# A linear-attention pair on one core: one more copy goes through the staging ring, one PSUM bank changes its ring, the launch's idle matmuls read a constant, and the order is fitted anew

## The chip, the core and the metric

The kernel runs on one core of a Trainium2 chip. The time is device microseconds of one execution, and the median of the runs is compared. The core has a matmul engine (TensorE, PE in the profile, whose weight loads are listed apart as PEld), three engines for element-wise work (VectorE is DVE, ScalarE is ACT, GpSimd is POOL), and queues that start transfers (SP is SyncE's; the other engines have queues of their own). Each engine runs its instructions strictly in the order in which they were written; they wait for one another by semaphores.

## The reference

Two independent blocks, A and B, each with its own `x` (2048 x 640), `wqkv` (640 x 1920) and `wo` (640 x 640), 32 heads of 20; the two results stand side by side in the output (2048 x 1280):

```python
q, k, v = split_heads(x @ wqkv)
phi = lambda t: jnp.where(t > 0, t + 1, jnp.exp(t)) + 1e-6
pq, pk = phi(q), phi(k)
kv = jnp.einsum("bhsd,bhse->bhde", pk, v)
z = jnp.einsum("bhsd->bhd", pk)
num = jnp.einsum("bhqd,bhde->bhqe", pq, kv)
den = jnp.einsum("bhqd,bhd->bhq", pq, z)[..., None] + 1e-6
out = merge_heads(num / den) @ wo
```

There is no softmax: keys and values meet in a 20 x 20 matrix per head, so `x` need not be multiplied by the value weights. The kernel forms G = phi(k)^T x first, then kv from G, then M = kv · wo, so that the output is (phi(q) / den) @ M.

## The kernel before, in words

**Arithmetic.** Every fp32 operand is split by a pair of passes into a high part (`xnh`, `kah`, `pkh` ..., written by ACT) and a low remainder (`xnl`, `kal`, `pkl` ..., written by DVE); a product is then three matmuls, high·high, low·high and high·low (`mm3`, lines 183 to 185, and `product`, line 333).

**First half: keys (about 0 to 290 us).** x comes in tiles of 128 rows. For each, phi(k) is found and G is added up. The projections of keys go by pairs of tiles in seven products (`STEPS`, `product`), as a block-matrix scheme that saves one product of eight; the first six tiles are projected plainly (`psk`, line 594). A product's results lie in PSUM banks "a" (`pa`), "e" (`pe`) and "one" (`psb`). ACT copies `pa` out (`ko`, line 337), DVE adds the others to it (line 340), and then follow exp (ACT), relu (ACT), min-and-add (`ek`, DVE, line 553), the high part `pkh` (ACT, line 565) and the low part `pkl` (DVE, line 569). Four tiles make a group; `gsum` multiplies the group's `pk` with its rows `xn` into a bank `psg` (seven sums, five of 512 columns and strips of 384 and 256), and DVE adds these to `gacc`. The column sums z of phi(k) are gathered by accumulating transfers (`zd`, line 561). `xn` is the row-wise load of x (`load_x`, line 406), in a ring "xr" of five buffers that it shares with `xt`, the transposed load from which `kah` and `kal` are cut.

**Between the blocks (159 to 200 us).** While block B's keys begin, block A's kv is made head group by head group: `kvmm` (`pskv`, line 776), a mask (`kvt`, line 783), its split (`kvh`, `kvl`), then `mmm` multiplies it with `wo` into two banks `psm` (80 or 120 rows), `m_out` copies both out to `mev` by ACT (line 337), and POOL stores them to DRAM as `md` (line 844). There are six head groups per block, four of 120 rows and two of 80.

**Second half: queries (about 290 to 562 us).** Eight units of 512 rows: Q by `psq`, phi(q), the denominators (`denmm`, bank `psd`, for the first and the last unit; sums by transfers for the rest), division, and `outmm` with M in the same seven products.

**What sets the order.** In the first half every step of PE and every piece of work beside it (a "job": a copy, a split, a load, a store) has a place, a number that follows from which step it feeds; `MOVED` shifts steps and `SHIFT` shifts jobs by a table of numbers, and all are then written out in the order of the places, dependencies first. In the second half `at` hangs work behind a matmul of Q or a product of the output, and `AT` shifts it by so many slots. A buffer is one of a ring named by its tag; its next user waits for the last reader of the user before it, a transfer included.

**What the change touches.** `m_out` takes `mev` of block A from ring "ek" (three buffers of pool `kg`, shared with `ek`) at this line:

```python
pool, tag, bufs = (q2[0], "o", 4) if q2 else (kg[0], "ek", 3)
```

Ring "wst" is the staging ring of seven buffers in pool `base` (`stage`): weights, `wv`, `wo` and later `md` are loaded into it. `bank` hands out PSUM banks by tag. At the launch, before any data is there, seven matmuls of bf16 on `idle`, a tile that DVE has zeroed (line 1108), go into a bank `psi` that nobody reads (line 1111).

Of the kernel before, what the change touches and what calls it, by code (L numbers as in the profile page):

```python
# [14 lines left out]
H = 32  # L15
# [7 lines left out]
    ('exp', 11): 0.74, ('exp', 13): 3.23, ('exp', 14): 0.41, ('exp', 15): 0.95, ('exp', 16): 0.91, ('exp', 18):  # L23
    -0.02, ('exp', 20): -0.96, ('exp', 22): 1.7, ('exp', 25): 0.96, ('exp', 28): 1.07, ('exp', 29): 0.86, ('exp',
    3): 4.78, ('exp', 4): 0.16, ('exp', 6): 0.87, ('exp', 8): -0.31, ('exp', 9): 2.13, ('f1', 'k', 0, 1): 0.31,
    ('f1', 'k', 1, 0): -0.71, ('f1', 'm', 0, 0): 1.2, ('f1', 'm', 0, 1): -0.83, ('f2', 'k', 0, 1): 2.5, ('f2', 'm',
    0, 0): 0.42, ('f5', 'k', 0): -0.1, ('f5', 'k', 1): -2.28, ('fdh', 'k', 1, 2): 0.51, ('fdh', 'k', 1, 4): 0.91,
# [10 lines left out]
    ('gacc', 7, 1): 0.04, ('gacc', 7, 4): 0.45, ('gacc', 7, 5): 1.7, ('gacc', 7, 6): 2.69, ('iota', 0): 0.8, ('kt',
    0): 0.53, ('kt', 1): 1.13, ('kt', 5): 5.23, ('kvh', 0): 1.2, ('kvh', 1): 5.9, ('kvh', 4): 1.1, ('kvl', 1): 2.02,
    ('kvl', 3): 2.08, ('ld', 'k', 1, 0): 0.56, ('ld', 'k', 1, 1): -0.06, ('ld', 'k', 1, 3): -9.42, ('ld', 'k', 1,  # L40
    4): -3.84, ('ld', 'm', 0, 0): 1.22, ('ld', 'm', 0, 1): 0.8, ('ld', 'm', 0, 2): 1.54, ('ld', 'm', 0, 3): -0.03,
    ('ld', 'm', 0, 4): -0.19, ('mc', 4, 1): 0.69, ('mix', 11): 0.24, ('mix', 12): 0.49, ('mix', 13): 7.61, ('mix',
    14): 4.05, ('mix', 15): -0.8, ('mix', 19): 1.66, ('mix', 2): -0.07, ('mix', 20): 0.31, ('mix', 23): 0.53,
# [1550 lines left out]
```

## Time and profile before

| | us |
|---|---|
| median of 3 runs | 568.26 (568.25 to 568.28) |
| the profiled execution | 567.32 |
| its span, first to last instruction | 565.2 |
| PE busy | 560.1 (99%) |
| PEld busy | 512.0 (91%) |
| DVE busy | 423.8 (75%) |
| ACT busy | 329.5 (58%) |
| POOL busy | 84.4 (15%) |

The profiled execution is 0.94 us shorter than the median of the runs, and 2.1 us of it lie outside the span. PE's time counts a matmul as busy up to a modelled end, so the distance from one matmul's start to the next one's says more than the busy share. A row of the timeline gives the start, the duration, the engine, the line, the operation with output<-inputs, and in brackets how long the engine had been idle before it and what ended that; where a row covers several instructions, xN says how many.

### The profile page before, as it was taken

What the parts mean: (1) busy time and instruction counts of PE and PEld (TensorE: products, weight loads), DVE (VectorE), ACT (ScalarE), POOL (GpSimd) and SP (SyncE); (2) the same over time, 40 slices, a digit from 0 to 9 for tenths busy, and PEclk for the clock granted to TensorE, in tenths of its full rate; (3) what the DMA queues carried; (4) which work ended last, traced back from release to release, by engine and by line L of the source; (5) the groups of instructions that cost most, each with busy time, mean ns of one, the idle gap of its engine ahead of it and who ended that gap; (6) DMA issues with size and microseconds to landing.
All of it is one profiled execution on the core that took longest, in us unless ns stands there. A gap on an engine that the chain in (4) does not pass through costs nothing.

```text
span 565.2 us, 9089 instructions
## 1 busy us (share of the span) xinstructions
PE 560.1 (99%) x3231; PEld 512.0 (91%) x3231; DVE 423.8 (75%) x729; ACT 329.5 (58%) x619; POOL 84.4 (15%) x141
## 2 busy tenths in 40 slices
PE   9999999999999999999999999999999999999997
PEld 7989999898989898989888899898989989898997
DVE  5987798886584878878855896968679485676892
ACT  5964676663575775666736764745547363454551
POOL 0111122311011112143110103121012101001010
PEclk9999999999999999999999999999999999999999
DMA  8969789999894787989998986846566994433022
GB/s 278 254 144 252 166 233 306 294 309 357 297 237 121 193 247 127 362 226 247 335 277 292 333 262 215 286 137 227 154 215 233 297 380 135 156 86 111 1 94 93
DMA packets 78613, 126.74 MB, mean 224 GB/s; under 512 B 9768, under 2 KB 40872, under 8 KB 78568
## 3 DMA queue, kind: packets, MB, share of 16 engines
q1 hardware_dynamic: 66120, 86.28, 47.3%
q0 software_dynamic: 12160, 39.66, 26.0%
q8 instruction: 25, 0.41, 0.3%
q10 hardware_dynamic: 288, 0.23, 0.1%
q14 instruction: 20, 0.16, 0.1%
HBM read 73.62 MB, written 49.37 MB: 218 GB/s over the span
## 4 chain that ended last, share of the span: by engine, by line
PE 96%; ACT 1%; DMA 1%; issue 0%; DVE 0%; POOL 0%; DVEq 0%; ACTq 0%
PE pa L333 22%; PE pe L333 11%; PE psq L183 8%; PE psq L185 8%; PE psq L184 8%; PE psg L184 8%; PE psg L185 8%; PE psg L183 8%; PE psb L333 7%; PE psk L594 5%; PE pskv L776 2%; DMA md<-mev 1%; PE psi L1111 1%; PE psm L183 1%; PE psm L185 1%; PE psm L184 1%
## 5 line engine op out<-in xcount | busy, mean ns | idle before, releaser
L183 PE MATMUL psq<-xqh,wqh 128*128 128x512 f32 x200 | 78.4, 392 | 0.0
L185 PE MATMUL psq<-xqh,wql 128*128 128x512 f32 x200 | 78.0, 390 | 0.0
L184 PE MATMUL psq<-xql,wqh 128*128 128x512 f32 x200 | 77.9, 389 | 0.0
L183 PE MATMUL psg<-pkh,xnh 128*128 128x512 f32 x160 | 62.8, 393 | 0.0
L184 PE MATMUL psg<-pkl,xnh 128*128 128x512 f32 x160 | 62.7, 392 | 0.0
L185 PE MATMUL psg<-pkh,xnl 128*128 128x512 f32 x160 | 62.6, 392 | 0.0
L337 ACT ACTIVATE o<-pa 128x320 f32<-128x320 f32 x64 | 28.1, 439 | 53.8 <-PE pa L333 53.6
L561 POOL DMA_DIRECT2D zd<-ek x30 | 26.1, 871 | 134.9 <-DVE ek L553 55.5
L185 PEld LDWEIGHTS psq<-xqh,wql 128*128 128x128 f32 x200 | 37.5, 188 | 7.9
L337 ACT ACTIVATE ko<-pa 128x320 f32<-128x320 f32 x52 | 22.5, 434 | 37.6 <-PE pa L333 37.4
L184 PEld LDWEIGHTS psq<-xql,wqh 128*128 128x128 f32 x200 | 37.6, 188 | 7.3
L183 PEld LDWEIGHTS psq<-xqh,wqh 128*128 128x128 f32 x200 | 37.6, 188 | 7.3
L944 ACT ACTIVATE pq<-psq 128x512 f32<-128x512 f32 x40 | 23.7, 594 | 28.0 <-PE psq L185 27.8
L185 PEld LDWEIGHTS psg<-pkh,xnl 128*128 128x128 f32 x160 | 30.0, 188 | 6.4
L998 DVE SCALAR_TENSOR_TENSOR pq<-pq,rd 128x1280 f32<-128x1280 f32 x16 | 23.4, 1483 | 16.2 <-DMA rd<-da 16.1
L184 PEld LDWEIGHTS psg<-pkl,xnh 128*128 128x128 f32 x160 | 30.1, 188 | 5.8 <-DVE pkl L569 0.5
L183 PEld LDWEIGHTS psg<-pkh,xnh 128*128 128x128 f32 x160 | 30.0, 188 | 5.2
L946 DVE SCALAR_TENSOR_TENSOR pq<-pq,rq 128x512 f32<-128x512 f32 x40 | 27.4, 686 | 8.4 <-ACT rq L945 8.4
L565 ACT ACTIVATE pkh<-ek,epst 128x640 fp32r<-128x640 f32 x32 | 26.5, 836 | 10.6 <-DVE ek L553 10.5
L553 DVE SCALAR_TENSOR_TENSOR ek<-ek,ko 128x640 f32<-128x640 f32 x32 | 26.2, 819 | 7.8 <-ACT ko L550 6.6
L639 DVE TENSOR_TENSOR gacc<-psg,gacc 128x512 f32<-128x512 f32 (+2 forms) x42 | 25.6, 627 | 6.7 <-PE psg L185 6.6
L340 DVE TENSOR_TENSOR o<-pe,o 128x320 f32<-128x320 f32 x32 | 15.3, 479 | 20.4 <-PE pe L333 13.5
(213 smaller groups left out, 1666.2 us busy)
## 6 DMA issues: line engine op xcount, KB each, us to landing
zd<-ek POOLq DMA_DIRECT2D x32, 320.0 KB, 5.3
out<-o POOLq DMA_DIRECT2D x28, 320.0 KB, 3.4
xql<-xd SPq DMA_DIRECT2D x24, 256.0 KB, 4.6
xt<-in_B_xt_tiles SPq DMA_DIRECT2D x16, 320.0 KB, 4.9
xn<-in_B_x SPq DMA_DIRECT2D x16, 320.0 KB, 5.6
xqs<-in_A_xt SPq DMA_DIRECT2D x20, 256.0 KB, 6.2
xqs<-in_B_xt SPq DMA_DIRECT2D x20, 256.0 KB, 5.7
fdmh<-fsh POOLq DMA_DIRECT2D x14, 320.0 KB, 4.5
```

Source lines behind the costliest of these rows:

```text
L183: nc.tensor.matmul(o, whi, xhi, start=first, stop=False)
L184: nc.tensor.matmul(o, whi, xlo, start=False, stop=False)
L185: nc.tensor.matmul(o, wlo, xhi, start=False, stop=last)
L333: nc.tensor.matmul(o, x, y, start=start and m == r == 0, stop=m == len(terms) - 1 and r == 2, skip_group_check=True)
L337: nc.scalar.activation(x, y, AF.Copy)
L553: nc.vector.scalar_tensor_tensor(ek[n], ek[n], 1.0, rk[n], op0=OP.min, op1=OP.add)
L561: nc.gpsimd.dma_start(zacc[b], e, accum_op=OP.add)
L565: nc.scalar.activation(pk[n][0], ek[n], AF.Identity, bias=epst)
L594: nc.tensor.matmul(kps["c", n][h], plain_x(n, c)[i], plain_w(c)[j][:, h * HF:(h + 1) * HF], start=(c == 0 and i == j == 0), stop=(c == NC ...
L639: nc.vector.tensor_tensor(o, x, o, op=OP.add)
L944: nc.scalar.activation(e, ps, AF.Exp)
L946: nc.vector.scalar_tensor_tensor(e, e, 1.0, r, op0=OP.min, op1=OP.add)
```

## The change

Three edits, and tables that were fitted again with them:

1. `m_out` takes block A's `mev` from the staging ring "wst" (seven buffers) instead of ring "ek" (three).
2. PSUM tag "small" (one bank, used by `psi` and `psd`) is gone; "one" has four banks instead of three, and `psi` and `psd` are taken from it. The total stays eight.
3. The idle matmuls read a bf16 constant 1.0 that the framework has in memory instead of `idle`; the tile and its memset go. `psi` is not read, so its value does not matter.
4. `SHIFT`, `MOVED` and `AT` have other numbers (some 300 entries in all; a few rows stand below).

```diff
@@ SHIFT, MOVED and AT: the core of it
 SHIFT = {
-    ('c0', 10): 1.79, ('c0', 11): 0.04, ('c0', 12): 0.56, ('c0', 3): 1.17, ('c0', 6): 0.26, ('c0', 7): 0.57, ('c0',
+    ('c0', 10): 1.79, ('c0', 12): 0.56, ('c0', 6): 0.26, ('c0', 7): 1.33, ('c0', 8): 0.25, ('c0', 9): 2.23, ('c2',
...
 MOVED = {
-    ('G', 2, 5): 2.0, ('G', 6, 0): 4.0, ('H', 3, 0, 0): 3.5, ('T', 1): 1.5, ('c', 2, 3): -3.0, ('m', 4): 3.0, ('p',
-    11, 3): -0.5, ('p', 13, 2): 1.0, ('p', 14, 0): -0.5, ('p', 14, 2): -2.0, ('p', 6, 1): 3.5, ('p', 7, 1): -1.0,
-    ('p', 7, 2): -2.5, ('p', 8, 4): -1.5, ('p', 9, 3): 2.0,
+    ('G', 2, 5): 2.0, ('G', 6, 0): 4.0, ('H', 3, 0, 0): 3.5, ('H', 7, 2, 2): 1.5, ('c', 2, 3): -2.5, ('c', 3, 3):
+    0.5, ('m', 5): -2.5, ('p', 13, 2): 1.0, ('p', 14, 0): -0.5, ('p', 14, 2): -2.0, ('p', 3, 6): -1, ('p', 6, 1):
+    3.5, ('p', 7, 1): -1.0, ('p', 7, 2): -2.5, ('p', 8, 4): -1.5, ('p', 9, 3): 2.0,
 }
...
     def bank(name, tag="one"):
-        return psums.tile([P, 512], F32, name=name, tag=tag, bufs={"one": 3, "a": 2, "e": 2, "small": 1}[tag])
+        return psums.tile([P, 512], F32, name=name, tag=tag, bufs={"one": 4, "a": 2, "e": 2}[tag])
...
         if h == 0:
-            pool, tag, bufs = (q2[0], "o", 4) if q2 else (kg[0], "ek", 3)
+            pool, tag, bufs = (q2[0], "o", 4) if q2 else (base, "wst", 7)
             mps[b, g, 2] = pool.tile([r, 2, HF], F32, name="mev", tag=tag, bufs=bufs)
...
     def denmm(u):
         t = acc.pop(u)
-        ps = den.pop(u) if u in den else bank("psd", "small")
+        ps = den.pop(u) if u in den else bank("psd")
...
     open_pool(kg, "kg", "left")
     open_pool(kx, "kx", "right")
-    idle = kg[0].tile([P, P], BF16, name="idle", tag="ek", bufs=3)
-    nc.vector.memset(idle, 0.0)
-    ps = bank("psi", "small")
+    idle = nc.const_aps.tensor(1.0, (P, P), BF16)
+    ps = bank("psi")
     for i in range(7):
```

The tables are 13 lines shorter, so a line number of the rows below is 13 smaller after the change (337 becomes 324).

**ScalarE where the fifth head group's M is copied out (about 194 to 198 us).** `mev<-psm 80x320 x2` are the two copies of that group, `ko<-pa` the copies of a key product's bank, `kah` and `ksh` high parts for the next products. Before:

```order
L337 ACTIVATE mev<-psm 120x320 x2
L550 ACTIVATE ko<-ko 128x640
L429 ACTIVATE kah<-xt 128x128
L805 ACTIVATE woh<-wo 80x640
L429 ACTIVATE ksh<-sx 128x512
L565 ACTIVATE pkh<-ek,epst 128x640 x2
L337 ACTIVATE ko<-pa 128x320
L337 ACTIVATE mev<-psm 80x320 x2
L337 ACTIVATE ko<-pa 128x320
```

and after:

```order
L537 ACTIVATE ko<-ko 128x640
L324 ACTIVATE mev<-psm 120x320 x2
L416 ACTIVATE kah<-xt 128x128
L792 ACTIVATE woh<-wo 80x640
L416 ACTIVATE ksh<-sx 128x512 x2
L552 ACTIVATE pkh<-ek,epst 128x640 x2
L324 ACTIVATE mev<-psm 80x320 x2
L324 ACTIVATE ko<-pa 128x320
L416 ACTIVATE ksh<-sx 128x512
L324 ACTIVATE ko<-pa 128x320
```

The 80-row copies now stand one copy of `pa` earlier. The first of them waited before for PE and for a transfer of a POOL queue (the store of an earlier `mev`, whose buffer in "ek" it takes); after, it waits for PE alone, since the buffer of "wst" that it takes was last read by DVE.

**TensorE in the last group's sums, at the third of the four tiles that it takes up (about 274 us).** `psg` are the banks of these sums, `pkh_3393` and `pkl_3394` (after: `pkh_3391` and `pkl_3392`) the two parts of that tile's phi(k), `xnh` and `xnl` those of its rows of x. Before:

```order
L183 MATMUL psg_3386<-pkh_3393,xnh_3308 128x512
L184 MATMUL psg_3386<-pkl_3394,xnh_3308 128x512
L185 MATMUL psg_3386<-pkh_3393,xnl_3309 128x512
L183 MATMUL psg_3396<-xnh_3308,pkh_3393 128x384
L184 MATMUL psg_3396<-xnl_3309,pkh_3393 128x384
L185 MATMUL psg_3396<-xnh_3308,pkl_3394 128x384
```

and after:

```order
L170 MATMUL psg_3394<-xnh_3310,pkh_3391 128x384
L171 MATMUL psg_3394<-xnl_3311,pkh_3391 128x384
L172 MATMUL psg_3394<-xnh_3310,pkl_3392 128x384
L170 MATMUL psg_3384<-pkh_3391,xnh_3310 128x512
L171 MATMUL psg_3384<-pkl_3392,xnh_3310 128x512
L172 MATMUL psg_3384<-pkh_3391,xnl_3311 128x512
```

The strip of 384 columns now comes first, so that the low part is wanted by the third matmul instead of the second.

**VectorE while block A's kv is masked (about 162 to 166 us).** `kvt` is a masked kv, `kvl` its low part, `pkl` the low parts of the first two tiles whose group sums PE takes up next. Before:

```order
L553 SCALAR_TENSOR_TENSOR ek_2003<-ek_2003,ko_1889 128x640
L173 TENSOR_TENSOR ksl_2018<-sx_1988,ksh_2017 128x512
L173 TENSOR_TENSOR kvl_2032<-kvt_2027,kvh_2031 120x120
L783 TENSOR_TENSOR kvt_2047<-pskv_2040,mask6_884 120x120
L173 TENSOR_TENSOR kal_1961<-xt_1822,kah_1960 128x512
L553 SCALAR_TENSOR_TENSOR ek_2037<-ek_2037,ko_1888 128x640
L783 TENSOR_TENSOR kvt_2067<-pskv_2061,mask4_887 80x80
L569 SCALAR_TENSOR_TENSOR pkl_2058<-ek_2003,pkh_2057 128x640
L569 SCALAR_TENSOR_TENSOR pkl_2073<-ek_2037,pkh_2072 128x640
```

and after:

```order
L160 TENSOR_TENSOR kvl_1986<-kvt_1983,kvh_1985 120x120
L540 SCALAR_TENSOR_TENSOR ek_2005<-ek_2005,ko_1884 128x640
L160 TENSOR_TENSOR ksl_2019<-sx_1988,ksh_2018 128x512
L160 TENSOR_TENSOR kvl_2033<-kvt_2028,kvh_2032 120x120
L770 TENSOR_TENSOR kvt_2051<-pskv_2044,mask6_882 120x120
L160 TENSOR_TENSOR kal_1954<-xt_1817,kah_1953 128x512
L540 SCALAR_TENSOR_TENSOR ek_2041<-ek_2041,ko_1883 128x640
L770 TENSOR_TENSOR kvt_2068<-pskv_2062,mask4_885 80x80
L556 SCALAR_TENSOR_TENSOR pkl_2058<-ek_2005,pkh_2057 128x640
L770 TENSOR_TENSOR kvt_2084<-pskv_2078,mask4_885 80x80
L556 SCALAR_TENSOR_TENSOR pkl_2076<-ek_2041,pkh_2075 128x640
```

One `kvl` has come to stand ahead of these rows and one mask multiply between the two `pkl`; both stood behind them before.

Two more places, in words. At about 209 to 212 us two `pkl` stood together before, behind an `ek`, the add of `pe` and a `kal` of 512 columns; after, the first stands ahead of all three, and the second alone behind them. And at about 50 us the load of A's rows 896 to 1023 (`xn` of tile 7) took a buffer of ring "xr" that a `kal` of 128 columns had freed; after, it takes the one of `xn` of tile 4, whose `xnl` stands on DVE right behind the add of a bank `psb`. On SyncE's queue the load stands in both between two loads of B's key weights.

More of the change, by code (lines that the diff above doesn't have):

```diff
@@ L19 @@
 SHIFT = {
[3 rows of a table removed]
[L23 to L27, printed above, removed]
@@ L28 @@
-    ('fdh', 'k', 1, 6): 0.53, ('fdh', 'm', 0, 7): 0.62, ('fdh', 'm', 0, 8): 0.57, ('fdl', 'k', 1, 1): 0.84, ('fdl',
[6 rows of a table removed]
-    ('fl', 'm', 0, 8): 1.99, ('gacc', 0, 1): 3.2, ('gacc', 1, 0): 2.35, ('gacc', 1, 3): 2.05, ('gacc', 2, 1): 2.89,
-    ('gacc', 2, 3): 0.28, ('gacc', 3, 1): 2.86, ('gacc', 3, 2): 2.86, ('gacc', 3, 3): 3.83, ('gacc', 3, 5): 2.14,
-    ('gacc', 4, 0): 0.75, ('gacc', 4, 4): 2.17, ('gacc', 5, 3): 1.28, ('gacc', 5, 5): 0.51, ('gacc', 7, 0): 0.31,
-    ('gacc', 7, 1): 0.04, ('gacc', 7, 4): 0.45, ('gacc', 7, 5): 1.7, ('gacc', 7, 6): 2.69, ('iota', 0): 0.8, ('kt',
@@ L39 @@
[L39 to L43, printed above, removed]
@@ L44 @@
-    ('mix', 26): 0.21, ('mix', 29): 2.2, ('mix', 3): -0.55, ('mix', 5): 7.49, ('mix', 7): 1.18, ('mix', 8): 4.49,
[16 rows of a table removed]
-    11): 0.09, ('relu', 13): 1.06, ('relu', 21): 4.46, ('relu', 25): 2.55, ('relu', 28): 1.48, ('relu', 30): 3.49,
[13 rows of a table removed]
-    ('wol', 4): 0.03, ('wqh', 1): 2.01, ('wql', 2): -0.55, ('wql', 4): 2.4, ('xh', 10, 'A1'): -0.17, ('xh', 10,
[13 rows of a table removed]
+    ('c0', 10): 1.79, ('c0', 12): 0.56, ('c0', 6): 0.26, ('c0', 7): 1.33, ('c0', 8): 0.25, ('c0', 9): 2.23, ('c2',
+    4): 0.43, ('c2', 8): 1.19, ('c2', 9): 0.48, ('c4', 15): 0.21, ('c5', 12): 0.75, ('c5', 3): 0.07, ('c5', 6):
@@ new lines @@
+    1.78, ('c5', 8): 1.02, ('exp', 0): 2.55, ('exp', 11): 0.74, ('exp', 13): 3.23, ('exp', 15): 0.61, ('exp', 16):
+    0.91, ('exp', 20): -0.96, ('exp', 22): 1.7, ('exp', 25): 0.96, ('exp', 28): 1.07, ('exp', 29): 1.23, ('exp', 3):
+    3.4, ('exp', 4): 2.25, ('exp', 6): 1.17, ('exp', 8): -0.31, ('exp', 9): 2.13, ('f1', 'm', 0, 0): 1.2, ('f1',
+    'm', 0, 1): -0.83, ('f2', 'k', 0, 1): 3.88, ('f2', 'm', 0, 0): 0.42, ('f5', 'k', 0): -2.36, ('f5', 'k', 1):
+    -2.28, ('fdh', 'k', 1, 2): 0.51, ('fdh', 'k', 1, 4): 0.91, ('fdh', 'k', 1, 6): 0.53, ('fdh', 'm', 0, 7): 0.57,
@@ new lines @@
+    ('fdl', 'k', 1, 1): 0.84, ('fdl', 'k', 1, 8): 1.97, ('fdl', 'm', 0, 2): 1.2, ('fdl', 'm', 0, 3): 0.76, ('fdl',
[5 rows of a table added]
+    ('gacc', 2, 1): 2.89, ('gacc', 3, 1): 2.86, ('gacc', 3, 2): 2.64, ('gacc', 3, 3): 3.78, ('gacc', 3, 5): 2.12,
+    ('gacc', 4, 0): 0.75, ('gacc', 4, 4): 2.17, ('gacc', 5, 3): 1.28, ('gacc', 5, 5): 0.51, ('gacc', 7, 0): 0.31,
+    ('gacc', 7, 5): 2.76, ('gacc', 7, 6): 1.79, ('iota', 0): 0.8, ('kt', 0): 1.7, ('kvh', 0): 1.2, ('kvh', 4): 1.1,
+    ('kvl', 1): 2.02, ('kvl', 3): 6.46, ('ld', 'k', 1, 0): 0.9, ('ld', 'k', 1, 1): -0.06, ('ld', 'k', 1, 3): -9.42,
@@ new lines @@
+    ('ld', 'k', 1, 4): -2.83, ('ld', 'm', 0, 1): 0.8, ('ld', 'm', 0, 3): -0.03, ('ld', 'm', 0, 4): -0.19, ('mc', 4,
+    1): 0.69, ('mix', 11): 0.24, ('mix', 12): 0.49, ('mix', 13): 7.61, ('mix', 14): 1.67, ('mix', 15): -0.8, ('mix',
+    17): 0.16, ('mix', 19): 1.66, ('mix', 20): 0.31, ('mix', 23): 1.04, ('mix', 29): 2.2, ('mix', 3): -0.55, ('mix',
[13 rows of a table added]
+    ('q6', 9): 0.96, ('relu', 1): 0.93, ('relu', 10): 1.37, ('relu', 11): 0.09, ('relu', 13): 1.06, ('relu', 21):
+    3.97, ('relu', 25): 2.55, ('relu', 28): 1.48, ('relu', 30): 3.62, ('relu', 5): 1.82, ('s1', 10): -0.46, ('s1',
[10 rows of a table added]
@@ L89 @@
+    9, 'h'): -5.5, ('woh', 4): 0.48, ('wol', 0): 0.5, ('wol', 3): 0.37, ('wol', 4): 0.03, ('wq', 4): -4.51, ('wqh',
[13 rows of a table added]
     'S3'): 2.46, ('xl', 8, 'A1'): 0.25, ('xl', 8, 'A5'): 1.23, ('xl', 8, 'S1'): 0.8, ('xl', 8, 'S3'): 1.04, ('xl',
[3 rows of a table removed]
[2 rows of a table added]
 }
 MOVED = {
[3 rows of a table removed]
[3 rows of a table added]
 }
@@ L102 @@
     ('a_split', 1, 0): 2, ('a_split', 2, 0): -1, ('a_split', 3, 0): -1, ('a_split', 5, 0): 2, ('a_split', 6, 0): 7,
-    ('d_split', 1, 0): 7, ('d_split', 1, 1): 5, ('d_split', 3, 1): -5, ('d_sums', 1, 0): 4, ('divide', 1, 0): 1,
-    ('divide', 2, 0): 1, ('divide', 5, 0): 1, ('form_last', 'm', 1): 5, ('form_load', 0, 5): -2, ('form_load', 1,
-    1): -2, ('form_load', 1, 5): -1, ('form_split', 'm', 1, 0): 5, ('form_split', 'm', 1, 1): -4, ('form_split',
-    'm', 1, 2): -3, ('form_split', 'm', 1, 3): -11, ('form_split', 'm', 1, 8): 3, ('form_split', 'm', 1, 9): 5,
-    ('form_sums1', 'm', 1, 1): -5, ('gather', 5): 4, ('invert', 3): -1, ('invert', 5): 3, ('kv_step', 1, 5): -2,
-    ('load_w', 'q', 1, 0): -3, ('load_w', 'q', 1, 4): 8, ('m_step', 1, 2): 1, ('m_step', 1, 3): 1, ('split_o', 1,
-    5): -2, ('split_w', 1, 0): -3, ('split_w', 1, 2): -7, ('split_w', 1, 4): 1,
+    ('d_split', 1, 1): 5, ('d_sums', 1, 0): 4, ('denmm', 0): -1, ('divide', 1, 0): 1, ('divide', 2, 0): 1,
+    ('form_last', 'm', 1): 5, ('form_split', 'm', 1, 0): 5, ('form_split', 'm', 1, 1): -4, ('form_split', 'm', 1,
+    2): -3, ('form_split', 'm', 1, 3): -11, ('form_split', 'm', 1, 8): 3, ('form_split', 'm', 1, 9): 5,
+    ('form_sums1', 'm', 1, 1): -5, ('invert', 3): -1, ('kv_step', 1, 5): -2, ('load_w', 'q', 1, 4): 8, ('m_step', 1,
+    2): 1, ('m_step', 1, 3): 1, ('split_w', 1, 0): -3, ('split_w', 1, 2): -7, ('split_w', 1, 4): 1,
 }
```

96 rows, old and new, of the table SHIFT are left out of this document.

## The prediction

> **What bounds the kernel now.** I read the page first, then PE's busy time by stretches of the span, then PE's waits, the chain of waits, and last PE's timeline at the gaps. PE is the bound:
>
> ```profile
> PE 560.1 (99%) x3231; PEld 512.0 (91%) x3231; DVE 423.8 (75%) x729; ACT 329.5 (58%) x619; POOL 84.4 (15%) x141
> ```
>
> ```profile
> core 0: us, PE busy (x) PEld busy (x) DVE busy (x) ACT busy (x) POOL busy (x), PEclk, DMA share, GB/s
> ...
> 32.00:285.00 253.00, 252.23 (x1473) 231.55 (x1472) 198.87 (x373) 158.62 (x289) 52.18 (x80) 1.00 0.88 248
> ...
> 304.00:532.00 228.00, 228.00 (x1251) 205.94 (x1251) 170.91 (x251) 126.81 (x233) 26.75 (x49) 1.00 0.61 206
> ```
>
> In the second half (304 to 532) PE has no idle time at all, in the first half (32 to 285) 0.77 us. The number of matmuls does not change, so all that the change can give lies in PE's few gaps. Two of them are named among its waits; the longest one inside stands on the chain as a transfer:
>
> ```profile
> PE psi L1111 <- DVE idle L1108: 1.0, 1, 1.0
> PE pa L333 <- ACT mev L337: 0.7, 1, 0.7
> ```
>
> ```profile
> 190.60 6.03 DMA md<-mev
> ...
> 332.60 1.76 PE pa L333 x12
> ```
>
> The second line gives the normal distance between matmuls of 320 columns, 1.76 / 12 = 0.147; for 512 columns it is 0.23 (rows at 165.83 and 166.06 below). Since idle time hides under modelled ends, I measure a gap as start to start, less that distance.
>
> **The change, part by part.**
>
> *`mev` in the staging ring.* ACT and PE at the gap:
>
> ```profile
> 196.73 0.76 ACT L337 ACTIVATE mev<-psm 80x320 f32<-80x320 f32 x2 [1.94 <-DMA md<-mev]
> ```
>
> ```profile
> 196.25 0.31 PE L333 MATMUL pa<-wfh,ksl 128*128 128x320 f32 x1
> 197.22 0.41 PE L333 MATMUL pa<-wfh,kah 128*128 128x320 f32 x1 [0.66 <-ACT mev L337]
> 197.47 0.30 PE L333 MATMUL pa<-wfl,kah 128*128 128x320 f32 x1
> ```
>
> The copy waited until the store of an earlier `mev`, issued at 190.60, had landed, and PE waited for the bank. PE loses 0.97 - 0.147 = 0.82, and the matmul behind a wait comes 0.25 after it instead of 0.147, another 0.10: 0.92 in all. After the change that store no longer owns the slot. What is late next: ACT had nothing to do for 1.94 before 196.73, so the pair could begin at 194.8 and end at 195.6, 0.8 before PE's turn at 196.25 + 0.15. The new slot was last read by DVE's split of `wo`, long ago; the next users of "wst" are the loads of `md`, which wait for all these stores anyway. POOL's store starts earlier and nobody waits for it there. So -0.92, between -0.92 and 0 (if another reader holds the slot).
>
> *Two `pkl` set apart, and the strip first.*
>
> ```profile
> 210.77 1.55 DVE L569 SCALAR_TENSOR_TENSOR pkl<-ek,pkh 128x640 fp32r<-128x640 f32 x2
> ...
> 212.12 0.40 PE L183 MATMUL psg<-pkh,xnh 128*128 128x512 f32 x1
> 212.38 0.50 PE L184 MATMUL psg<-pkl,xnh 128*128 128x512 f32 x1
> 212.72 0.40 PE L185 MATMUL psg<-pkh,xnl 128*128 128x512 f32 x1
> ```
>
> ```profile
> 273.95 0.82 DVE L569 SCALAR_TENSOR_TENSOR pkl<-ek,pkh 128x640 fp32r<-128x640 f32 x1 [0.90 <-ACT pkh L565]
> ...
> 274.49 0.40 PE L183 MATMUL psg<-pkh,xnh 128*128 128x512 f32 x1
> 274.83 0.50 PE L184 MATMUL psg<-pkl,xnh 128*128 128x512 f32 x1
> 275.17 0.40 PE L185 MATMUL psg<-pkh,xnl 128*128 128x512 f32 x1
> ```
>
> At 212 PE loses 0.60 - 0.46 = 0.14 to a `pkl` that ends at 212.32. One `pkl` now precedes in DVE's idle time, so the last ends some 0.7 earlier: -0.14. At 274 PE loses 0.68 - 0.46 = 0.22. With the strip first, `pkl` is wanted after two matmuls of 384 columns instead of one of 512, by the ratio of columns 2 x 0.17 = 0.34 instead of 0.23 later, just when it is ready (274.77): -0.22, at worst -0.11.
>
> *A copy behind a load.*
>
> ```profile
> 206.14 0.74 ACT L473 ACTIVATE xnh<-xn 128x640 fp32r<-128x640 f32 x1 [0.26 <-DMA xn<-in_B_x]
> ...
> 208.90 0.42 ACT L337 ACTIVATE ko<-pa 128x320 f32<-128x320 f32 x1
> ...
> 209.10 0.40 PE L185 MATMUL psg<-pkh,xnl 128*128 128x512 f32 x1
> 209.38 0.42 PE L333 MATMUL pa<-wfh,kah 128*128 128x320 f32 x1
> 209.63 0.31 PE L333 MATMUL pa<-wfl,kah 128*128 128x320 f32 x1
> ```
>
> PE loses 0.05 + 0.10 = 0.15 behind a copy that a load delayed by 0.26. The loads around it stand further apart in the new order, so I take -0.15; if the load lands no sooner while PE arrives 0.92 earlier, it is up to +0.77 instead.
>
> *A kv mask and a `kvl` ahead of a `pkl`.* This is the one place where the new order costs something that I can see:
>
> ```profile
> 162.07 0.28 DVE L173 TENSOR_TENSOR kvl<-kvt,kvh 120x120 fp32r<-120x120 f32 x1
> 162.26 0.27 DVE L783 TENSOR_TENSOR kvt<-pskv,mask 120x120 f32<-120x120 f32 x1
> ...
> 163.79 0.23 DVE L783 TENSOR_TENSOR kvt<-pskv,mask 80x80 f32<-80x80 f32 x1
> 163.94 1.65 DVE L569 SCALAR_TENSOR_TENSOR pkl<-ek,pkh 128x640 fp32r<-128x640 f32 x2
> ```
>
> ```profile
> 165.83 0.39 PE L184 MATMUL psg<-pkl,xnh 128*128 128x512 f32 x1
> 166.06 0.39 PE L185 MATMUL psg<-pkh,xnl 128*128 128x512 f32 x1
> ```
>
> The second `pkl` ends at 165.59. At 212 a `pkl` that ended at 212.32 held PE as if its matmul had begun at 212.49, 0.17 later; here that is 165.76, 0.07 before the turn. A `kvl` takes 0.19 of DVE (162.07 to 162.26) and a mask multiply 0.15 (163.79 to 163.94): 0.34 more, less 0.07, is +0.27; with the mask alone +0.08. I take +0.20.
>
> *The launch.* PE's first matmul waited 1.0 for the zeroed tile; without it, PE may start sooner, by less than that. But its work soon waits for data:
>
> ```profile
> 7.57 0.29 ACT L176 ACTIVATE kah<-x 128x128 fp32r<-128x128 f32 x1
> 7.92 0.56 PE L594 MATMUL psk<-wh,kah 128*128 128x320 f32 x2
> ```
>
> The matmul at 7.92 follows at once a split (7.57 + 0.29 = 7.86) that hangs on loads: what PE wins ahead of it is waited away. So 0; bounds 0 and -0.1, one wait's aftermath. [...]
>
> *The banks.* PE's waits name no `psd` or `psq`, and PE is never idle in the second half. Four banks in one ring instead of three and one: 0, with +0.1 if the last unit's `psd` delays a `psb`. The `AT` moves and the tail: 0, with PE's unbroken work as their cover.
>
> The sum: -0.92 - 0.14 - 0.22 - 0.15 + 0.20 = -1.23. Against the profiled execution that is 567.32 - 1.23 = 566.1 (565.2 of it is now span, 2.1 around it). The median of the runs stands 0.94 above the profiled one, and the change gives 568.26 - 1.23 = 567.0. A measurement of this kernel can tell about 0.2% (1.14 us) from no change; the forecast lies just beyond that.
>
> **The rivals.**
>
> *A load comes later than its copy needs it (slower).* The load of tile 7's rows gets another buffer:
>
> ```profile
> 50.57 0.33 SPq L406 DMA_DIRECT2D xn<-in_A_x  x1
> ...
> 52.42 0.49 DVE L340 TENSOR_TENSOR ko<-psb,ko 128x320 f32<-128x320 f32 x1 [1.92 <-PE psb L333]
> ...
> 57.02 0.74 ACT L473 ACTIVATE xnh<-xn 128x640 fp32r<-128x640 f32 x1 [0.27 <-DMA xn<-in_A_x]
> 58.95 0.44 ACT L337 ACTIVATE ko<-pa 128x320 f32<-128x320 f32 x1 [1.20 <-PE pa L333]
> ...
> 61.16 0.44 ACT L337 ACTIVATE ko<-pa 128x320 f32<-128x320 f32 x1 [0.22 <-PE pa L333]
> ...
> 62.34 0.31 PE L333 MATMUL pa<-wfh,ksh 128*128 128x320 f32 x1
> ```
>
> ```profile
> DMA to landing us min/median/max: 3.1/5.1/8.7
> ```
>
> It was issued at 50.57 and used at 57.02, 6.45 later. After, its buffer is freed by an `xnl` behind the add at 52.42: 52.9 + 0.8 (a DVE pass of 640 columns) = 53.7. ACT can take 1.20 + 0.22 of delay, and PE's matmul at 62.34 another 0.7 past the copy at 61.16 (ends 61.60): it must land by 57.02 + 2.1 = 59.1, within 5.4. At the median of all `xn` loads it does. With its own 6.45 it costs 1.05 + 0.10, and the sum is about -0.1: no change, 568.2. At 8.7 it costs 3.4: 570.4. It decides for slower from a landing of 5.4 + 2.3 = 7.7 on. For it speaks that transfers are busy 0.88 of that stretch, against it that SyncE has issued nothing for some 4 us by then. [...] The load of 206.14 is a second place of the same kind.
>
> *The wait only moves.* If the slot in "wst" is held, or ACT's row comes late for another reason, PE still waits at 197: the sum without the first term is -0.31, 567.9.
>
> *The kv place costs its full price and the small gains do not come.* -0.92 + 0.27 = -0.65: 567.6.
>
> **How the numbers follow.** Forecast 0.60, of which 0.48 beyond -1.14 and 0.12 short of it; a load that is late by up to some 2 us, the wait that only moves and the small gains lost, together 0.18, all within 0.2%; slower by a load near the top of its landing times, here or at 206, 0.22. Faster 0.48, same 0.30, slower 0.22. The range begins at 566.2 (the sum with +0.20 gone, the launch's -0.1 and 0.5 from moves that I did not price) and ends at 569.3, between a landing of 6.45 and one of 8.7; outside it I leave 0.2.
>
> **What would show it.** After the change the chain has no `md<-mev` near 190, PE's waits do not name `mev`, and the starts at 196 to 197 run on at 0.15. Near 274 three matmuls of 384 columns come first, with no distance above 0.25. At about 166 a matmul on `pkl` comes some 0.2 late. A first matmul well before 1.0 and an unchanged one near 7.9 show the launch right. I am wrong if ACT's `xnh` or a `ko<-pa` stands behind a transfer for more than 1.5 us near 60 or 205, or if a wait that is not in the old trace stands on the chain.

## The result and the profile after

| | before | after |
|---|---|---|
| median of 8 runs of each, us | 568.19 (566.68 to 569.24) | 566.26 (565.61 to 566.99) |
| ratio, 95% interval | | 0.997 [0.9958, 0.9981] |
| the profiled execution, us | 567.32 | 566.22 |
| its span, us | 565.2 | 564.4 |
| time outside the span, us | 2.1 | 1.8 |

The change makes the kernel 1.93 us faster, by the interval 1.1 to 2.4. The two profiled executions differ by less, 1.10, since that of before was a short one: 0.87 below the median of its kernel, that of after 0.04 below. The ratios here and below are worked out from the single runs, without three executions of 930 to 1978 us, and so need not be the ratios of the medians.

The page's first part and PE's busy time by stretches, after. The columns of the second are those that the prediction shows:

```profile
PE 560.2 (99%) x3231; PEld 512.1 (91%) x3231; DVE 424.1 (75%) x728; ACT 329.0 (58%) x619; POOL 84.4 (15%) x141
```

```profile
32.00:285.00 253.00, 252.94 (x1478) 232.19 (x1477) 201.04 (x376) 161.19 (x295) 52.23 (x80) 1.00 0.88 250
...
304.00:532.00 228.00, 228.00 (x1253) 206.00 (x1252) 171.18 (x251) 126.09 (x233) 26.76 (x49) 1.00 0.61 203
```

PE's idle time between 32 and 285 us has fallen from 0.77 to 0.06; the second half is as full as it was. Of PE's waits one is left, of 0.8 at the launch.

ACT and PE where the fifth group's M is copied out, after:

```profile
193.62 0.74 ACT L324 ACTIVATE mev<-psm 80x320 f32<-80x320 f32 x2
```

```profile
196.52 0.31 PE L320 MATMUL pa<-wfh,kah 128*128 128x320 f32 x1
196.67 0.31 PE L320 MATMUL pa<-wfl,kah 128*128 128x320 f32 x1
```

The copy waits for no transfer, and PE's starts run on at 0.15: the 0.92 of before is gone. The places where the prediction expected a loss or a remainder, PE after, at 166, 274 and (not expected) 264 us:

```profile
165.56 0.39 PE L170 MATMUL psg<-pkh,xnh 128*128 128x512 f32 x1
165.83 0.50 PE L171 MATMUL psg<-pkl,xnh 128*128 128x512 f32 x1
166.17 0.40 PE L172 MATMUL psg<-pkh,xnl 128*128 128x512 f32 x1
...
263.81 0.40 PE L171 MATMUL psg<-pkl,xnh 128*128 128x512 f32 x1
264.15 0.50 PE L172 MATMUL psg<-pkh,xnl 128*128 128x512 f32 x1
264.48 0.40 PE L170 MATMUL psg<-pkh,xnh 128*128 128x512 f32 x1
...
274.06 0.44 PE L172 MATMUL psg<-xnh,pkl 128*128 128x384 f32 x1
274.34 0.40 PE L170 MATMUL psg<-pkh,xnh 128*128 128x512 f32 x1
```

Against the usual 0.23 between matmuls of 512 columns (and 0.17 of 384), PE loses 0.04 + 0.11 at 166, 0.11 + 0.10 + 0.04 at 264 (the last from 264.95 to 265.22) and 0.11 at 274. Measured in this way, start to start, the profiled pair differs as follows:

| place, us | before | after | after - before |
|---|---|---|---|
| launch, up to the start near 8.7 (8.63 and 8.76) | | | +0.13 |
| 28 | 0.10 | 0 | -0.10 |
| 156 | 0.37 | 0.32 | -0.05 |
| 166 | 0 | 0.15 | +0.15 |
| 196 to 197 (`mev`) | 0.92 | 0 | -0.92 |
| 209 (copy behind a load) | 0.15 | 0 | -0.15 |
| 212 (`pkl`) | 0.14 | 0 | -0.14 |
| 264 | 0 | 0.25 | +0.25 |
| 274 (strip first) | 0.22 | 0.11 | -0.11 |
| sum | | | -0.94 |

The spans differ by 0.8, and what lies around the spans by 0.3.

### The profile page after: what moved, and what is told of

Same layout as the page of the kernel before. It is cut to its first block, busy times and chain, and to the rows that moved or that the text cites. A ratio compares the mean times of both kernels' runs of the same rounds, so it can differ in the third digit from the quotient of the medians.

```text
span 564.4 us, 9087 instructions
## 1 busy us (share of the span) xinstructions
PE 560.2 (99%) x3231; PEld 512.1 (91%) x3231; DVE 424.1 (75%) x728; ACT 329.0 (58%) x619; POOL 84.4 (15%) x141
## 4 chain that ended last, share of the span: by engine, by line
PE 99%; ACT 1%; DVE 0%; issue 0%; DVEq 0%
PE pa L320 22%; PE pe L320 11%; PE psg L172 8%; PE psg L171 8%; PE psg L170 8%; PE psq L170 8%; PE psq L172 8%; PE psq L171 8%; PE psb L320 7%; PE psk L581 5%; PE pskv L763 2%; PE psm L170 1%; PE psm L172 1%; PE psm L171 1%; PE psi L1097 1%; PE pst L641 0%
## 5 line engine op out<-in xcount | busy, mean ns | idle before, releaser
L416 ACT ACTIVATE ksh<-sx 128x512 fp32r<-128x512 f32 x26 | 16.2, 628 | 24.6 <-DVE sx L434 24.3
```

## The experiments

The prediction's large term is the wait of `mev`. My theory at the start was: the ring alone removes it and gives some 0.9 us, and the tables do the small rest. One rival was that the wait only moves; another that the fitted tables and the ring need each other. The first four kernels put the ring, the tables and the three edits apart. Each kernel is compared with runs of before made beside it on the same chip; the medians of before there were 567.68 (first four), 567.78 (next four) and 567.41 (last four).

| kernel | median us | ratio to before, 95% |
|---|---|---|
| e1_ring_only | 568.04 | 1.001 [0.9995, 1.0025] |
| e2_ring_back | 570.21 | 1.0044 [1.003, 1.0058] |
| e5_three_edits | 568.01 | 1.0009 [0.9994, 1.0023] |
| e6_before_again | 567.71 | 0.9996 [0.9985, 1.0006] |
| e9_ring_and_load | 568.25 | 1.0011 [1.0, 1.0021] |
| e3_const_only | 567.50 | 0.9995 [0.9984, 1.0007] |
| e4_banks_only | 567.44 | 0.9998 [0.9986, 1.001] |
| e8_three_waits | 565.56 | 0.9959 [0.9942, 0.9975] |
| e10_ring_and_z | 567.21 | 0.9989 [0.9979, 0.9999] |
| e12_ring_z_load | 565.94 | 0.9972 [0.9961, 0.9983] |
| e11_z_late | 568.27 | 1.0004 [0.9992, 1.0016] |
| e14_after_again | 565.95 | 0.997 [0.9958, 0.9981] |

### e1: the ring alone

The kernel before, with one line changed:

```diff
-            pool, tag, bufs = (q2[0], "o", 4) if q2 else (kg[0], "ek", 3)
+            pool, tag, bufs = (q2[0], "o", 4) if q2 else (base, "wst", 7)
```

> The kernel before with one edit: block A's mev from the staging ring instead of ring ek. My theory: the wait of ScalarE for md<-mev near 190 to 197 is gone, TensorE's starts run on at 0.15 there, and the kernel is 0.9 us faster than before (0.6 to 1.2), about half of what the whole change gave (1.9). Rival, the wait only moves (another reader or ScalarE's row holds TensorE at the same place): 0, within 0.3. Rival, the wait in a typical execution is longer than in the profiled one: 1.5 to 1.9 faster.

No gain: 1.001. PE's waits no longer name `mev`, but a wait on `ko` has come:

```profile
PE pa L333 <- ACT ko L337: 1.4, 2, 1.3
```

It stands 12 us further on. Behind it, followed back from PE over ACT and DVE to SyncE, in e1:

```profile
209.94 0.41 PE L333 MATMUL pa<-wfh,kah 128*128 128x320 f32 x1 [1.26 <-ACT ko L337]
```

```profile
206.08 0.74 ACT L473 ACTIVATE xnh<-xn 128x640 fp32r<-128x640 f32 x1 [1.01 <-DMA xn<-in_B_x]
207.34 0.83 ACT L565 ACTIVATE pkh<-ek,epst 128x640 fp32r<-128x640 f32 x1 [0.52 <-DVE ek L553]
...
209.47 0.42 ACT L337 ACTIVATE ko<-pa 128x320 f32<-128x320 f32 x1
```

```profile
204.48 0.84 DVE L724 STREAM_TRANSPOSE zt<-zs 128x640 f32<-128x640 f32 x1 [1.94 <-DMA zs<-zd]
...
206.49 0.81 DVE L553 SCALAR_TENSOR_TENSOR ek<-ek,ko 128x640 f32<-128x640 f32 x1
```

```profile
197.60 0.43 SPq L720 DMA_DIRECT2D zs<-zd  x1
```

The same two rows of `zs` in before, where DVE did not wait:

```profile
197.45 0.42 SPq L720 DMA_DIRECT2D zs<-zd  x1
```

```profile
203.21 0.84 DVE L724 STREAM_TRANSPOSE zt<-zs 128x640 f32<-128x640 f32 x1
```

`zs` is A's sum of phi(k) read back from DRAM; DVE transposes it into `zt` and adds it up, and nobody is in a hurry for that. But on DVE's row the `ek` of a tile stands behind it, on ACT's row the `pkh` of that `ek` and then the copy of `pa` for which PE waits. Ahead of that `pkh`, ACT also waits for the rows of tile 23 (`xn`). Two late transfers lie on the same path. PE loses 1.43 (209.94 less 208.28, the start ahead of it, less 0.23) and the usual 0.10 behind a wait: more than the 0.92 won. The second wait of the two on `ko` stands at 234 and costs 0.34 + 0.10. The theory falls; "the wait only moves" holds, though the place is another than the one I had given.

### e2: the changed kernel with the old ring

```diff
-            pool, tag, bufs = (q2[0], "o", 4) if q2 else (base, "wst", 7)
+            pool, tag, bufs = (q2[0], "o", 4) if q2 else (kg[0], "ek", 3)
```

> The kernel after with one edit undone: mev back in ring ek. My theory: the wait for a store of mev returns, and of the 1.9 us that the change gave, 0.9 are lost: 1.0 faster than before (0.6 to 1.4). Rival, the fitted order had already moved the copies off the store: 1.9 faster, as the whole change. Rival, the order was fitted to the new ring, so that in the old one the wait is longer than before: 0 or slower.

Slower than before, 1.0044, and by its ratio some 0.7% slower than the changed kernel. ACT and PE in e2:

```profile
197.16 0.76 ACT L324 ACTIVATE mev<-psm 80x320 f32<-80x320 f32 x2 [3.08 <-DMA md<-mev]
197.81 0.43 ACT L324 ACTIVATE ko<-pa 128x320 f32<-128x320 f32 x1
```

```profile
198.29 0.41 PE L320 MATMUL pa<-wfh,ksh 128*128 128x320 f32 x1 [2.13 <-ACT ko L324]
```

The order after puts the copies of M one copy of `pa` earlier (the rows of the order ahead of the prediction). With the old ring they wait 3.08 for the store and hold that copy behind them: PE loses 2.29 (198.29 less 195.85, less 0.15). The store took as long as in before (the copy starts 6.09 after the store's issue at 191.07; in before 6.13 after 190.60); only what is queued behind the waiting copy is more urgent. So the tables count on the ring. The granted clock fell to 0.50 after this gap, as the stretch from 200 to 201 us of e2 shows in its third figure from the end:

```profile
200.00:201.00 1.00, 1.00 (x6) 1.00 (x5) 0.60 (x2) 0.60 (x1) 0.00 (x0) 0.50 0.92 207
```

### e5: the three edits with the old tables

The kernel before, with the diff's edits 1, 2 and 3 and no entry of a table changed.

> The kernel before with the three edits and none of the new numbers in the tables. My theory: 0.9 us faster than before, all of it from mev; launch and banks give 0 (within 0.1 each). Rival, the tables give nothing and the edits all: 1.9 faster. Rival, launch or banks cost something that the tables repaired: less than 0.5 faster.

No gain either, 1.0009. The timeline of e5 has the path of e1 once more, with the longest wait of all on DVE:

```profile
204.66 0.85 DVE L724 STREAM_TRANSPOSE zt<-zs 128x640 f32<-128x640 f32 x1 [2.68 <-DMA zs<-zd]
```

PE starts again at 210.12, 2.17 late, and here too runs at a granted clock of 0.50 for a while. The edits without the tables are worth nothing.

### e6: the kernel before once more

No edit; a second profile, to see which waits belong to the kernel and which to one execution.

> The kernel before once more, unchanged, for a second profile and the spread of one program against itself: ratio 1.000 within 0.0015. My theory on why the change gave 1.9 us by the medians and 1.1 by the two profiled executions: the first profiled execution of before was a quick one, and this profile has a span 0.5 to 1 us above 565.2, with the extra in waits for transfers (near 190 to 197, or in the first 10 us). Rival: the same span, and the extra lies outside the span.

0.9996. The wait of `mev` is there, but half as long, and another has come near 233. ACT's and PE's rows of e6:

```profile
196.01 0.76 ACT L337 ACTIVATE mev<-psm 80x320 f32<-80x320 f32 x2 [1.57 <-DMA md<-mev]
```

```profile
195.90 0.31 PE L333 MATMUL pa<-wfh,ksl 128*128 128x320 f32 x1
196.49 0.41 PE L333 MATMUL pa<-wfh,kah 128*128 128x320 f32 x1 [0.29 <-ACT mev L337]
```

Here PE loses 0.59 - 0.15 + 0.10 = 0.54 instead of 0.92. At 233 it loses 0.79 + 0.11, where it lost next to nothing in the first profile: ACT's split of a loaded piece of M waits for the load that waits for the stores of `mev` (1.78 at 231.16, against 0.51 at 230.76 in the first profile). So the size of these waits is a sample of one execution: 1.94 and 1.57 for `mev`, 0.51 and 1.78 for this split, in two profiles of one kernel.

### e9: the ring, and tile 23's load earlier

After e1 the first suspect was the load of tile 23's rows, since the prediction's term at 209 named it. In addition to e1's line:

```diff
-    ('n', 23): 2.26
+    ('n', 23): 0.5
```

> The ring edit alone (which gave nothing: TensorE then waited 1.4 us near 210 for a copy behind the load of tile 23's rows), and one load moved: the load of tile 23's rows stands right behind the load of xt 26 on SyncE's queue instead of behind three more transfers. Theory, that load's landing took back what the ring gave: it is issued 1.5 us earlier (near 197 instead of 198.5) and lands that much earlier, the wait near 210 falls from 1.4 to under 0.3, and the kernel is 0.8 to 1.3 us faster than before. Rival, the landing hangs on the traffic and not on the issue: it lands near 206 as before, and the time stays within 0.4 of before. Rival, the next load (md, used near 231) takes the gain: the wait near 210 is gone, one near 233 has grown, time within 0.4.

1.0011, no better than e1. The load is issued at 197.12 instead of 198.61, and ACT's `xnh` waits no more; but the next row takes over the whole wait. ACT and DVE in e9:

```profile
205.05 0.73 ACT L473 ACTIVATE xnh<-xn 128x640 fp32r<-128x640 f32 x1
207.30 0.83 ACT L565 ACTIVATE pkh<-ek,epst 128x640 fp32r<-128x640 f32 x1 [1.52 <-DVE ek L553]
```

```profile
204.44 0.84 DVE L724 STREAM_TRANSPOSE zt<-zs 128x640 f32<-128x640 f32 x1 [1.80 <-DMA zs<-zd]
```

PE starts again at 209.91, where it did in e1 (209.94). The theory of the single load falls, and so did the rivals that I had set beside it: none named `zs`. It is this row that led to it.

### e3 and e4: the launch and the banks, each alone

```diff
-    idle = kg[0].tile([P, P], BF16, name="idle", tag="ek", bufs=3)
-    nc.vector.memset(idle, 0.0)
+    idle = nc.const_aps.tensor(1.0, (P, P), BF16)
```

> The kernel before with one edit: the idle matmuls read the constant. My theory: 0 (within 0.4); the first matmul starts near 0.78 instead of 1.02, and the one near 7.9 starts where its data let it. [...] The part of the time outside the span (2.1 before, 1.8 to 1.85 in the runs of the ring edit and of the whole change) stays at 2.1 if it belongs to the ring edit.

```diff
-        return psums.tile([P, 512], F32, name=name, tag=tag, bufs={"one": 3, "a": 2, "e": 2, "small": 1}[tag])
+        return psums.tile([P, 512], F32, name=name, tag=tag, bufs={"one": 4, "a": 2, "e": 2}[tag])
...
-        ps = den.pop(u) if u in den else bank("psd", "small")
+        ps = den.pop(u) if u in den else bank("psd")
...
-    ps = bank("psi", "small")
+    ps = bank("psi")
```

> The kernel before with one edit: psd and psi in the common ring of PSUM banks, four instead of three. My theory: 0 (within 0.4), since no matmul waits for such a bank. Rival, a fourth bank lets the psg or psb steps begin earlier: 0.3 to 0.6 faster; rival, the last unit's psd delays a psb: up to 0.5 slower, to be seen between 532 and 562.

0.9995 and 0.9998: neither can be told from nothing. In e3 the first matmul starts at 0.78, and at 8.40 PE waits 0.9 for ACT's `kah`:

```profile
PE psk L594 <- ACT kah L176: 0.9, 1, 0.9
```

What PE wins at the start is waited away there, as the prediction's row at 7.92 suggested.

### e8: the changed kernel with three small waits moved

The gaps that were left at 156, 166 and 264 have a DVE or ACT piece in front of them that could stand elsewhere:

```diff
-    ('fl', 'm', 0, 5): 1.11
+    ('fl', 'm', 0, 5): 5.5
...
-    ('xh', 10, 'A1'): -0.17
+    ('xh', 10, 'A1'): 1.0
...
-    ('xl', 10, 'A1'): 4.35
+    ('xl', 10, 'A1'): 3.2
...
+    ('kt', 5): 5.23,
```

> The kernel after with four numbers of SHIFT changed, against its three largest gaps that are left: the kv mask near 165 goes back behind both pkl (0.16), the split of a form of M near 261 behind the two xnl (0.26), and the kah near 155 behind the copy of pa and a pkh (0.32). By my theory that gaps add up where nothing late stands behind them: 0.7 us less than the whole change, so 2.3 to 2.7 faster than before. Rival, what is won is waited away at a load, as with the ring alone: 1.5 to 2.1 faster, with a new wait at 209 or 231.

0.9959 [0.9942, 0.9975], the fastest of all, though the interval overlaps that of the changed kernel, so that it is not shown to be faster than that. The gaps at 156 and 264 are gone, and 0.11 is left at 166; a new one stands at 92:

```profile
91.69 0.31 PE L321 MATMUL pe<-wfh,ksl 128*128 128x320 f32 x1
92.16 0.41 PE L321 MATMUL pe<-wfh,ksh 128*128 128x320 f32 x1 [0.16 <-DVE ko L328]
```

It costs 0.32 + 0.10, which takes back most of the 0.32 + 0.25 won. Gaps of this size cannot be seen one by one in a median.

### e10 and e12: the ring, and `zs` earlier, without and with tile 23's load

e10 is e1 with the load of `zs` ahead of a load of keys' rows; e12 has e9's entry too:

```diff
-    ('zl',): 1.6
+    ('zl',): -1.0
```

> The ring edit alone, and the load of z's sums (zs) one place earlier on SyncE's queue, ahead of the load of xt 26. Theory after the last runs: not the load of tile 23 but this one took back what the ring gave; VectorE's transpose zt waits for it (1.8 to 2.7 us in the runs with the ring edit) and the ek that follows on VectorE is what TensorE lacks near 210. Issued near 195.8 instead of 197.6 it lands in time; what is left is the wait of xnh for tile 23 (1.0 with the ring alone), so the gap near 210 falls from 1.4 to 0.9 or less, and the time is 0.3 to 0.9 below the ring alone, 0 to 0.6 faster than before. Rival, the landing does not follow the issue: zt still waits over 1.5 us, time as with the ring alone.

> As the one before, and tile 23's load right behind that of xt 26 as well. Theory: now both transfers land in time, the gap near 210 is under 0.3, and the kernel is 0.6 to 1.4 faster than before; the load of md used near 231 may keep up to 0.5 of it. Rival, one more transfer comes late in their place (the two loads of xt behind them, or md): 0, within 0.3.

e10 is 0.9989, e12 0.9972: the ring and two moved loads, with the rest of the old tables, the old launch and the old banks, give the whole gain of the change. In e10 DVE's transpose waits no more, and ACT's `xnh` does, 0.49 for the rows of tile 23 (its profiled execution, at 568.72 the longest of its twelve, also has a wait of PE on ACT's `pkh`, 1.2, that PE's waits in e12 and e1 do not name). In e12 neither waits. SyncE, DVE, ACT and PE in e12:

```profile
195.95 0.32 SPq L720 DMA_DIRECT2D zs<-zd  x1
...
197.11 0.42 SPq L406 DMA_DIRECT2D xn<-in_B_x  x1
```

```profile
202.54 0.84 DVE L724 STREAM_TRANSPOSE zt<-zs 128x640 f32<-128x640 f32 x1
```

```profile
205.05 0.73 ACT L473 ACTIVATE xnh<-xn 128x640 fp32r<-128x640 f32 x1
```

```profile
208.37 0.39 PE L185 MATMUL psg<-pkh,xnl 128*128 128x512 f32 x1
208.60 0.31 PE L333 MATMUL pa<-wfh,kah 128*128 128x320 f32 x1
```

PE runs on at 0.23 where e1 lost 1.53. The earlier load of tile 23 alone gives nothing (e9), the earlier `zs` alone about 0.1% (e10), both together the whole: each is hidden behind the other's wait. No run has the two moved loads with the old ring and the old tables, so what the ring is worth beside them was not measured apart; e2 has the old ring only with all the new tables.

### e11: the changed kernel with `zs` late

```diff
-    ('zl',): 0.73
+    ('zl',): 2.6
```

> The kernel after with one number changed: the load of z's sums stands two places later on SyncE's queue, behind the load of tile 23, so that it is issued near 199.1 instead of 195.8. Theory: zt waits some 3 us, ek and pkh come late, TensorE gets a gap of 1.5 to 2.5 near 209 and, where it is over 2, some 3 us at half clock behind it: 1.5 to 3.5 slower than the kernel after, so 0.4 faster to 1.6 slower than before. Rival, the kernel after owes its gain to something else than this load: no change against after, 1.5 to 2.2 faster than before.

1.0004: this one entry takes the whole gain away. SyncE, DVE and PE in e11:

```profile
198.37 0.55 SPq L707 DMA_DIRECT2D zs<-zd  x1
```

```profile
204.06 0.85 DVE L711 STREAM_TRANSPOSE zt<-zs 128x640 f32<-128x640 f32 x1 [2.11 <-DMA zs<-zd]
```

```profile
209.53 0.41 PE L320 MATMUL pa<-wfh,kah 128*128 128x320 f32 x1 [1.57 <-ACT ko L324]
```

With e12 it makes the case from both sides: the `zs` entry, together with that of tile 23, put in beside the ring gives the gain; the `zs` entry alone, taken out of the changed kernel, takes it. In the changed kernel `zs` is issued at 195.78, two places earlier on SyncE's row than here, and DVE's transpose at 202.60 waits for nothing:

```profile
195.78 0.37 SPq L707 DMA_DIRECT2D zs<-zd  x1
```

```profile
202.60 0.84 DVE L711 STREAM_TRANSPOSE zt<-zs 128x640 f32<-128x640 f32 x1
```

### e14: the changed kernel once more

> The kernel after once more, for a second profile and beside the others on one chip: 1.5 to 2.2 faster than before. If the gain is that its loads land in time, VectorE's zt and ScalarE's xnh of tile 23 again wait for no transfer, and no gap of TensorE behind the first 10 us is over 0.4.

0.997 [0.9958, 0.9981], as the first time, with a median 1.46 below that of before beside it. Neither `zt` nor tile 23's `xnh` waits for a transfer. Of the small gaps, 156 (0.33), 166 (0.16) and 274 (0.10) are there again; 264 has shrunk to 0.12. The launch reads otherwise:

```profile
5.36 0.31 PE L581 MATMUL psk<-wl,kah 128*128 128x320 f32 x1
...
7.86 0.56 PE L581 MATMUL psk<-wh,kah 128*128 128x320 f32 x2 [0.28 <-ACT kah L163]
```

The distance of 0.15 between matmuls begins at 5.36 (6.86 in the first profile of this kernel, 6.04 in that of before), and then PE waits for data. So the +0.13 of the first pair at the launch is one execution's, not the change's.

### How late `zs` may be

From DVE's transpose to PE's start behind the wait it is the same time wherever the transpose waits and PE behind it: 209.94 - 204.48 = 5.46 (e1), 209.91 - 204.44 = 5.47 (e9), 210.12 - 204.66 = 5.46 (e5), 209.53 - 204.06 = 5.47 (e11). Even a kernel with the old ring shows it once; DVE and PE in e4:

```profile
203.68 0.84 DVE L724 STREAM_TRANSPOSE zt<-zs 128x640 f32<-128x640 f32 x1 [0.81 <-DMA zs<-zd]
```

```profile
208.67 0.40 PE L185 MATMUL psg<-pkh,xnl 128*128 128x512 f32 x1
209.15 0.42 PE L333 MATMUL pa<-wfh,kah 128*128 128x320 f32 x1
```

209.15 - 203.68 = 5.47 again, with 0.25 + 0.10 lost. Where PE does not wait for it, its turn comes 6.06 after the transpose in e12, 5.93 in the changed kernel (208.53), 6.12 in the first profile of before (209.33), 5.59 in the second (208.60). So before had 0.66, 0.13 or less than nothing to spare. How `zs` fared, from the rows of its load and the landing that the view of this tile gives:

| kernel | issued | to landing, us | landed | DVE waited |
|---|---|---|---|---|
| before, e6, e3, e4 | 197.1 to 198.0 | 5.1, 5.9, 5.3, 6.0 | 202.6 to 203.7 | 0, 0.4, 0, 0.8 |
| e1, e9, e5 | 197.0 to 198.2 | 6.9, 6.2, 7.6 | 204.4 to 204.6 | 1.9, 1.8, 2.7 |
| e11 | 198.4 | 5.7 | 204.0 | 2.1 |
| after, e14, e8, e12 | 195.6 to 196.0 | 3.2, 5.6, 5.6, 2.8 | 198.8 to 201.5 | 0 |

e1's 1.43 against the first profile of before is then: 0.82 for PE's turn that came sooner (208.51 instead of 209.33), 1.27 for the transpose that came later (204.48 instead of 203.21), less the 0.66 that was to spare. The first of these is the removed wait coming back. The second is that the transfer took longer in all three kernels with the new ring and `zs` in its old place. In e1 the second store of `mev` is issued at 196.56, ahead of `zs`, in before at 197.79, behind it. With the old ring it went ahead of `zs` too in e6 (by 0.05) and e4 (by 0.24), where `zs` took 5.9 and 6.0, and behind it in e3, where it took 5.3; whether this order is why, no run tells apart.

## Why the prediction was right, and where not

**The forecast.** Faster by about 1.2 was forecast, 1.93 came (1.46 when the changed kernel was run once more, e14); 566.26 lies at the very end of the range, which begins at 566.2, 0.7 below the 567.0. In the profiled pair, on which the sum was worked out, it is 1.10 against 1.23. That this is so near is in part luck: PE's gaps gave 0.94 of the 1.23, 0.3 came from outside the span, where the sum had nothing, and the largest term came whole only through a moved load that the prediction did not look at.

**`mev`, -0.92: right in size, but not for the reason given.** The wait disappeared as said, and the copies had time. The step that failed is "What is late next": it looked at ACT's time before PE's next turn, 0.8, and there it was right. But the wait had held back what stands behind it: without it PE's turn near 209, 12 us further on, came 0.82 sooner (208.51 in e1, 209.33 in before), and the two transfers on which PE's work there hangs, issued at about 198, had been landing in that time. The ring alone gives 0 (e1), so that the term came whole was luck as far as the prediction's argument goes. The term holds only because the tables also moved loads: `zs` is issued 1.7 earlier (195.78 instead of 197.45), and a load of keys' rows that SyncE had sent right behind those of tile 23 (199.85) now goes ahead of them (196.21), and tile 23's rows land in 5.9 instead of 7.7 (whether for that reason wasn't tried by itself). Of this the prediction had only the second part, and priced it at 0.15. My rival "the wait only moves" had a fitting result, but named a held slot or ACT's row, not this.

**The copy behind a load, -0.15.** It came, and the bound that I gave for the other case, up to +0.77 "if the load lands no sooner while PE arrives 0.92 earlier", is the mechanism of e1 in one of its two halves. The other half, `zs`, stands in the trace of before only as a row without a wait, 203.21, with a landing some 0.6 ahead of it.

**`pkl` at 212, -0.14; the strip at 274, -0.22.** The first came whole. The second came by half, -0.11, its worst case: the third matmul of the strip, the one on the low part, still kept the next one waiting for 0.11.

**kv at 166, +0.20.** 0.15 in the first profile, 0.16 in the second. The second `pkl` ended 0.19 later (165.78 instead of 165.59), not the 0.34 worked out: PE and DVE came there 0.05 earlier, and of the mask's 0.15 some 0.10 fell into time in which DVE had waited between the two `pkl` (1.65 for the pair, 1.55 for the one at 210.77).

**Launch and banks, 0.** e3 and e4 agree.

**What was not foreseen.** 264: DVE's two `xnl` come late for PE, 0.25 in the first profile and 0.12 in the second. Outside the span 0.3 went: 2.06 to 2.18 us lie there in the runs of before, 1.81 to 1.90 in those of after. e4 stays at before's value (2.07 to 2.15); most other kernels here, e9 and e12 with the ring and moved loads among them, are at 1.73 to 1.91, whether they are faster than before or not, and e1 and e3 are spread from 1.77 to 2.09. Since e3 has the old ring, it isn't the ring alone. No row of a profile shows this part, and its cause is open.

**The gain beyond the sum.** 0.83 of the 1.93 is the difference between the profiled executions and their medians: the first profile was of a short one. e6, whose profiled execution took 567.71, within 0.03 of the median of before beside it, has 0.90 at 233 (with what comes behind the wait) that the first profile had not, and 0.38 less at `mev`; it also lost 0.39 near 446 and reached 28 us 0.35 sooner, so that its span is only 0.4 longer. In both profiles of after neither 233 nor `mev` waits. Of the nine profiles with the old tables, or these but for one or two loads, five lose 0.36 to 0.90 at 232 to 234 (e6, e4, e1, e9, e12); of the five with the new ones, after, e14, e8, e11 and e2, none does. No run takes this place apart from the rest. So the part of the gain that hangs on landings differs from one execution to the next, and a sum made against one of them can't give it.

**The slower rival did not come.** Its place was the load of tile 7's rows. It was issued where worked out, at 53.7, and ACT's split waited 0.46:

```profile
57.22 0.74 ACT L460 ACTIVATE xnh<-xn 128x640 fp32r<-128x640 f32 x1 [0.46 <-DMA xn<-in_A_x]
```

It landed after 3.5 us, near the 3.1 that is the shortest of all `xn` loads, far from the 7.7 at which it would have decided. The kind was right and the place wrong: a load that lands too late does decide this change, at 204 and not at 57, in e1, e9, e5 and e11.

## What to carry to other kernels

Before a wait is priced as a gain, list what else was under way while it lasted, for as far behind it as transfers take to land (here 2.8 to 7.7 us for `zs` and tile 23's rows): each transfer that lands close ahead of its reader, and each in-order row on which that reader stands before something urgent, is the next wait. Price such a slack even where the row shows no wait at all; here 0.66 us behind a row without a bracket decided whether 0.92 was won. And an edit that removes a wait and a table of places fitted with it are tried together and apart, since either half alone may give nothing (here the ring, 1.001) or lose (the tables with the old ring, 1.0044).
